# Opening an attention kernel over 256-row pieces of its input, with delayed value sums, the gate as a 129th value column, and four SSM input buffers

## The chip, the cores and the metric

The kernel runs on one core of a Trainium2 chip. The metric is the device time in microseconds (us) from start to end of one execution on that core; lower is better. Several executions of each kernel were timed.

Engines are named as the profile names them: PE is the matrix engine (TensorE), PEld its weight loads, DVE is VectorE, ACT is ScalarE, POOL is GpSimd, and SP is the engine that only starts DMA transfers here.

## The reference

A sequence `x` of 2048 rows and 1024 columns goes through two blocks, and a gate per row mixes their results.

```python
# x: 1 x 2048 x 1024, bf16
g = sigmoid((x * gate_w).sum(-1, keepdims=True))      # one gate value per row
a = A(x)      # state-space block (SSM): Bu = x @ B_bar.T (complex), h[t] = Lam_bar*h[t-1] + Bu[t],
              # y = 2*Re(h @ C.T) + x*Dskip; 2048 steps, 1024 complex states
b = B(x)      # attention: x @ wqkv, 32 heads of 32, softmax(q k^T / sqrt(32)) v, @ wo
out = g * a + (1 - g) * b                             # 1 x 2048 x 1024, bf16
```

The attention has 32 x 2048 x 2048 scores, and every one needs an exponential. That is 134 million exponentials on ScalarE.

## The kernel before

All exponentials are done in 1024 ACTIVATE instructions of 128 x 1024 elements. Two of them make a *burst*: the scores of one group of four heads, 256 query rows against 256 key rows. There are 512 bursts. Everything else (projections, the whole SSM block, the output projection) is cut into pieces and placed between the bursts: `MM_PER_PERIOD = 4` matmuls of 512 columns per burst on PE ("dense slots"), and VectorE work as long as a *planned* time says that there is room.

```python
def build(self):
    ...
    start = [self.d_v(0, 0), self.d_qk(0, 1, 1), self.d_v(0, 1), self.d_qk(0, 1, 2), self.d_v(0, 2), self.d_qk(0, 1, 3), self.d_v(0, 3),
             self.d_qk(0, 0, 1)]                      # V, K, Q of the first four heads: 512-column pieces, one bank
    proj[0] = [self.d_qk(0, 0, 2), self.d_gate(), self.d_qk(0, 0, 3)]
    ...
    for p in range(NBURST):
        g, pg = divmod(p, 64)
        self.burst(p)                                 # PE: scores; ACT: two exponentials
        if p >= 2:
            self.pv(p - 2)                            # PE: value sums of the burst before last
        ...
        quota = 8 if start else MM_PER_PERIOD
        ...                                           # dense pieces until the quota is used
        limit = t0 + (period - 0.1 if ended is not None else period + PE_HEAD)
        while self.bg or self.bg2:                    # VectorE background work, by planned time
            ...
            c = src[0][0]                             # planned cost of the next operation
            st = max(self.dve_t, t0 + 0.3)
            if c > 0 and st + c > limit:
                break
            src.pop(0)[1]()
            if c > 0:
                self.dve_t = st + c
        ...
        if ended is not None:
            ended.evac()                              # VectorE: PSUM -> SBUF, after the background work
            self.dve_t = max(self.dve_t, t0 + period) + 0.75
```

VectorE executes in the order in which the operations are emitted, as the runs below show: a K eviction emitted behind two operations of parameter math started 0.57 us after its matmuls were through (the changed kernel), and one emitted ahead of such math 0.04 us after (a_spareK).

The gate is computed by dense work of its own, with a moving operand that is one column wide:

```python
    def d_gate(self):
        ...
                for tt in (2 * q, 2 * q + 1):
                    for a in range(8):
                        m = e.matmul(ps[:, 7, tt:tt + 1], xT[:, a, 128 * tt:128 * (tt + 1)], self.gwb[:, a:a + 1], start=(a == 0), stop=(a == 7))
```

## Time and profile before

The time before is 978.16 us, the median of 3 executions (978.06 to 978.17).

The first lines are from the profile's page: busy time, share of the span and instruction count of each engine; the clock granted to PE in 40 equal slices, in tenths of full speed; and the chain of work that ended last, by engine.

```profile
...
PE 935.0 (96%) x15432; PEld 487.9 (50%) x15432; DVE 522.9 (54%) x1206; ACT 944.7 (97%) x1034; POOL 8.4 (1%) x46
...
PEclk9989999999999999999999999999999999999997
...
ACT 90%; DVE 5%; PE 3%; SPq 1%; DMA 0%; issue 0%
...
```

PE and ACT look equally busy, at 96% and 97%. The chain decides between them: 90% of it is ACT. Two slices of the clock row stand out: the third (an 8, between 49 and 73 us) and the last (a 7).

The next view divides the execution into four stretches: opening, the next 22 us, the long middle, and the tail after the start of the last exponential. The columns after the length are busy us and instruction counts of the engines, then the mean granted clock, the share of the DMA engines, and GB/s.

```profile
...
core 0: us, PE busy (x) PEld busy (x) DVE busy (x) ACT busy (x) POOL busy (x), PEclk, DMA share, GB/s
12.93:40.37 27.44, 22.51 (x353) 14.43 (x351) 23.52 (x92) 17.54 (x19) 2.45 (x6) 1.00 1.18 201
40.37:62.40 22.03, 20.31 (x396) 11.48 (x395) 20.73 (x78) 18.97 (x21) 0.00 (x0) 0.77 0.99 136
62.40:965.80 903.40, 877.30 (x14566) 454.27 (x14565) 472.04 (x1010) 903.16 (x986) 3.27 (x18) 1.00 0.23 54
965.80:976.90 11.10, 5.27 (x44) 1.95 (x40) 4.87 (x22) 2.83 (x6) 0.00 (x0) 0.50 0.23 78
...
```

ACT is busy for 903.16 of 903.40 us in the long middle. Nothing can be saved there unless an exponential becomes cheaper. What can be saved lies at the edges: ACT is idle for 9.9 us of the opening, for 3 us of the next stretch (at a mean clock of 0.77), before 12.93 us, and in the tail (at a clock of 0.50).

The opening's pattern shows in the timeline. Each line gives start and duration in us, engine, source line, operation, operands, count and, in brackets, how long the engine sat idle and what released it.

```profile
...
15.89 1.89 PE L1295 MATMUL f_ps<-f_xT,f_wb 128*128 128x512 bf16 x8 [0.79 <-DVE f_V L1319]
...
17.82 0.69 DVE L1302 CAST f_K<-f_ps 128x512 bf16<-128x512 f32 x1 [0.46 <-PE f_ps L1295]
...
18.57 0.40 PE L1448 MATMUL f_ps<-f_Q,f_K 32*128 32x256 bf16 x8 [0.79 <-DVE f_K L1302]
...
19.01 1.94 ACT L1454 ACTIVATE f_pt<-f_ps 128x1024 bf16<-128x1024 f32 x2 [1.92 <-PE f_ps L1448]
...
```

PE projects 512 columns of K (1.89 us), VectorE empties the bank (0.69 us), PE makes the scores, and only then can ACT go on, after 1.92 us of idleness. Then V follows (1.95 us at 19.31), with the same bank.

The clock dips between 45.05 and 55.29 us. The same view at its start:

```profile
...
43.36 0.40 PE L1448 MATMUL f_ps<-f_Q,f_K 32*128 32x256 bf16 x8
...
44.11 0.94 PE L1329 MATMUL f_ps<-f_gwb,f_xT 128*128 128x1 bf16 x32
...
45.12 0.61 PE L1448 MATMUL f_ps<-f_Q,f_K 32*128 32x256 bf16 x8
...
```

The scores (8 matmuls) take 0.40 us before 45.05 us and 0.61 us after it. The gate's matmuls, 128x1 each, run just before. The stretch view of the 3.41 us ahead of the drop is instructive:

```profile
...
41.64:45.05 3.41, 3.41 (x113) 2.81 (x112) 3.23 (x11) 3.41 (x5) 0.00 (x0) 1.00 1.43 176
...
```

PE was busy for 3.41 of 3.41 us there (by the profile, which models when a matmul ends), and still the clock was half (0.50) from its end to 55.29 us. What was low was the work in it: the one-column matmuls start 0.025 to 0.027 us apart, and 512-column ones at full clock 0.215 us apart. Counting the columns of the matmuls that start in that window, each matmul weighted by the share of the 128 rows that it used, it holds 1952 columns; 512-column matmuls one after the other would move about 8100 (estimate from the 0.215 us).

### The profile page before, as it was taken

How to read it: one execution, taken by the hardware profiler on the slowest of the kernel's cores; microseconds unless marked ns; L12 is line 12 of the kernel's file. 1: busy time of each engine (PE TensorE's matmuls, PEld its weight loads, DVE VectorE, ACT ScalarE, POOL GpSimd, SP SyncE). 2: the span in 40 equal slices, each digit the busy share in tenths (PEclk: the TensorE clock that was granted, in tenths of full speed). 3: DMA queues.
4: the chain of work that ended last, by engine and by line, in shares of the span. 5: the costliest groups of instructions: out<-in, count | busy, mean ns of one | idle time of the engine just before them, and what ended most of it. 6: DMA issues, size and time to landing. Idle time of an engine off the chain costs nothing.

```text
span 976.9 us, 33704 instructions
## 1 busy us (share of the span) xinstructions
PE 935.0 (96%) x15432; PEld 487.9 (50%) x15432; DVE 522.9 (54%) x1206; ACT 944.7 (97%) x1034; POOL 8.4 (1%) x46
## 2 busy tenths in 40 slices
PE   7899999999999999999999999999999999889996
PEld 4544554554444464444644644444554446444442
DVE  4897789877778844511257711177765112232223
ACT  4789999999999999999999999999999999999996
POOL 2000000000000000000000000000000000000000
PEclk9989999999999999999999999999999999999997
DMA  9992312311135202130022201142101213123311
GB/s 213 183 137 44 45 21 50 65 24 40 40 69 98 56 5 45 35 80 29 8 48 58 53 26 44 35 91 55 36 5 41 92 37 104 53 85 109 114 58 60
DMA packets 157011, 60.89 MB, mean 62 GB/s; under 512 B 145600, under 2 KB 145600, under 8 KB 156864
## 3 DMA queue, kind: packets, MB, share of 16 engines
q1 hardware_dynamic: 153664, 57.89, 26.8%
q8 instruction: 122, 2.00, 0.9%
q10 hardware_dynamic: 3200, 0.80, 0.4%
q14 instruction: 25, 0.20, 0.1%
HBM read 16.79 MB, written 12.58 MB: 30 GB/s over the span
## 4 chain that ended last, share of the span: by engine, by line
ACT 90%; DVE 5%; PE 3%; SPq 1%; DMA 0%; issue 0%
ACT f_pt L1454 90%; DVE f_OT L1218 1%; PE f_ps L1313 1%; DVE f_OT L1214 1%; PE f_ps L1470 1%; DVE f_OT L1216 1%; SPq L1020 0%; PE f_ps L1295 0%; PE f_ps L1448 0%; DVE f_OT L1215 0%; DMA f_xT<-in_A_x_dram 0%; PE f_ps L1344 0%; DVE f_V L1319 0%; DVE f_Et L1220 0%; DVE f_K L1302 0%
## 5 line engine op out<-in xcount | busy, mean ns | idle before, releaser
L1454 ACT ACTIVATE f_pt<-f_ps 128x1024 bf16<-128x1024 f32 x1024 | 940.7, 1266 | 13.7 <-PE f_ps L1448 13.6
L1470 PEld LDWEIGHTS f_ps<-f_V,f_pt 128*128 128x128 bf16 x8192 | 239.0, 96 | 110.0 <-issue 106.4
L1470 PE MATMUL f_ps<-f_V,f_pt 128*128 128x33 bf16 x8192 | 291.4, 178 | 0.5 <-DVE f_On L1484 0.5
L1448 PE MATMUL f_ps<-f_Q,f_K 32*128 32x256 bf16 x4096 | 204.2, 274 | 27.4 <-ACT f_pt L1454 8.0
L1448 PEld LDWEIGHTS f_ps<-f_Q,f_K 32*128 32x128 bf16 x4096 | 60.6, 92 | 246.1 <-ACT f_pt L1454 238.3
L1344 PE MATMUL f_ps<-f_xT,f_wb 128*128 128x512 bf16 x512 | 131.0, 377 | 2.4 <-DVE f_ub L1348 0.9
L1295 PE MATMUL f_ps<-f_xT,f_wb 128*128 128x512 bf16 x496 | 128.2, 382 | 2.3 <-DVE f_V L1319 1.3
L1383 DVE TENSOR_SCALAR f_Ag<-f_ps,f_gcol 128x512 f32<-128x512 f32 x32 | 24.0, 750 | 139.8 <-PE f_ps L1368 139.8
L1244 DVE TENSOR_TENSOR_SCAN f_ht<-f_pf,f_init,f_ut 128x512 bf16<-128x512 f32 x64 | 80.4, 1273 | 0.0
L1368 PE MATMUL f_ps<-f_cT_re,f_hp 128*128 128x512 bf16 x192 | 72.8, 379 | 0.3
L1368 PE MATMUL f_ps<-f_cT_im,f_hp 128*128 128x512 bf16 x192 | 72.6, 378 | 0.0
L1348 DVE CAST f_ub<-f_ps 128x512 bf16<-128x512 f32 x64 | 44.3, 691 | 51.9 <-PE f_ps L1344 51.8
L1313 PE MATMUL f_ps<-f_wb,f_xT 128*128 128x128 bf16 x1024 | 67.0, 219 | 0.0
L1401 PE MATMUL f_ps<-f_wb,f_OT 128*128 128x512 bf16 x252 | 65.9, 380 | 0.0
L1407 DVE SCALAR_TENSOR_TENSOR f_xT<-f_ps,f_gcol,f_hp 128x512 bf16<-128x512 f32 (+1 forms) x28 | 21.0, 751 | 76.2 <-PE f_ps L1401 76.2
L1313 PEld LDWEIGHTS f_ps<-f_wb,f_xT 128*128 128x128 bf16 x1024 | 57.6, 97 | 0.4 <-issue 0.2
L1344 PEld LDWEIGHTS f_ps<-f_xT,f_wb 128*128 128x128 bf16 x512 | 40.4, 96 | 34.5 <-issue 2.8
L1295 PEld LDWEIGHTS f_ps<-f_xT,f_wb 128*128 128x128 bf16 x496 | 39.4, 97 | 35.1 <-issue 2.1
L1302 DVE CAST f_Q<-f_ps 128x512 bf16<-128x512 f32 x31 | 21.4, 691 | 51.3 <-PE f_ps L1295 51.3
L1235 DVE TENSOR_TENSOR f_tq<-f_ub,f_Et 128x512 bf16<-128x512 bf16 x128 | 46.3, 419 | 0.1
L1235 DVE TENSOR_TENSOR f_tq<-f_ht,f_Et 128x512 bf16<-128x512 bf16 x128 | 46.3, 417 | 0.0
L1319 DVE CAST f_V<-f_ps 128x512 bf16<-128x512 f32 x32 | 22.2, 693 | 42.0 <-PE f_ps L1313 42.0
(114 smaller groups left out, 435.5 us busy)
## 6 DMA issues: line engine op xcount, KB each, us to landing
ag_scratch<-f_Ag SPq DMA_DIRECT2D x32, 256.0 KB, 2.0
f_hp<-ag_scratch SPq DMA_DIRECT2D x32, 256.0 KB, 2.7
f_wb<-in_B_wqkv_dram SPq DMA_DIRECT2D x21, 256.0 KB, 4.3
out_dram<-f_xT SPq DMA_DIRECT2D x16, 256.0 KB, 2.1
f_wb<-in_B_wo_dram SPq DMA_DIRECT2D x1, 1024.0 KB
f_OT<-f_On SPq DMA_TRANSPOSE x63, 2.4
f_wb<-in_B_wqkv_dram ACTq DMA_DIRECT2D x3, 256.0 KB, 3.8
f_wb<-in_B_wo_dram SPq DMA_DIRECT2D x1, 768.0 KB, 4.6
```

The lines of the kernel that those rows point to most:

```text
L1235: ops.append((c, lambda: dve(lambda e: e.tensor_tensor(o, a, b, op), r, w)))
L1244: ops.append((1.25, lambda ri=ri: dve(lambda e: e.tensor_tensor_scan(ht[:, ri, :], rr, ut[:, ri, :], self.init[:, ri, j:j + 1], ALU.mult, ...
L1295: mms.append((1, lambda e, f, l, a=a: e.matmul(ps[:, bank, :], w[:, g % 2, part, a, :], xT[:, a, 512 * ch:512 * (ch + 1)], start=f, stop=l ...
L1313: m = e.matmul(ps[:, bank, 128 * q:128 * (q + 1)], xT[:, a, 128 * kt:128 * (kt + 1)], w[:, g % 2, 2, a, :], start=(a == 0), stop=(a == 7))
L1344: mms.append((1, lambda e, f, l, a=a: e.matmul(ps[:, 7, :], bT[:, n % 2, ri, a, :], xT[:, a, 512 * ch:512 * (ch + 1)], start=f, stop=l), [ ...
L1348: self.dve(lambda e: e.tensor_copy(self.ub[:, n % 2, ri, :], ps[:, 7, :]), [("bank", 7)], [("ub", n % 2, ri)], "evac_u")
L1368: mms.append((1, lambda e, f, l, j=j, ri=ri: e.matmul(ps[:, 7, :], hp[:, ri, j, cols], cT[ri][:, j, 512 * cb:512 * (cb + 1)], start=f, sto ...
L1383: self.dve(lambda e: e.tensor_scalar(a, ps[:, 7, :], self.gcol[:, 0, tt:tt + 1], None, ALU.mult), [("bank", 7), "g0"], [at], "evac_c")
L1401: mms.append((1, lambda e, f, l, j=j: e.matmul(ps[:, 7, :], OT[:, j, 256 * qb + 128 * r:256 * qb + 128 * (r + 1)], wo[j][0][:, 512 * cb:51 ...
L1448: m = e.matmul(ps[:, 2 * sl[h // 2] + h % 2, 256 * kl:256 * (kl + 1)], K[32 * h:32 * h + 32, g % 2, 128 * kt:128 * (kt + 1)], Q[32 * h:32 ...
L1454: self.act(lambda e, s=s, p=p: e.activation(pt[:, p], ps[:, 2 * s:2 * s + 2, :], ACT.Exp, scale=SCALE), [("S", s)], [("pt", p)], "exp")
L1470: m = e.matmul(ps[:, 6, o:o + 33], pt[:, p, h2, 256 * kl + 128 * qt:256 * kl + 128 * (qt + 1)], V[:, g % 2, 2 * i + kl, h, :], start=(i == ...
```

## The change

The intent is to start ACT earlier and keep it fed, by five things:

1. K and V of the first four heads are projected in 256-row pieces, as `x` lands, so that bursts 0 to 8 can follow the pieces. All value sums are held back until burst 8 has been issued, so PE has less to do per piece. This needs 12 more tiles for exponentials, found in memory that is not used yet.
2. The gate weights become a 129th column of the value weights; the separate gate matmuls go.
3. Four instead of two input buffers (`ub`) for the first 16 SSM items.
4. The last four output matmuls ("rest") move from burst 508 to bursts 510 and 511, two in each.
5. The parameter math of the SSM is placed between the pieces of the opening, 0.7 us of it (planned) after each V eviction.

The core of the diff:

```diff
+REST = 510
...
-        self.ub = T("ub", [128, 2, 2, 512], BF)
+        ub = T("ub", [128, 2, 2, 512], BF)
+        self.ub = [ub[:, 0], ub[:, 1]] + [self.OT[:, 3, 1024 * k:1024 * (k + 1)].rearrange("p (r n) -> p r n", r=2) for k in range(2)]
...
-        for q in range(4):
-            self.ld_x(128 * q, 128 * (q + 1), ("x0", q))
-        for ch in range(1, 4):
-            self.ld_x(512 * ch, 512 * (ch + 1), ("x", ch))
...
+        self.ld_x(0)
...
+        for i in range(1, 8):
+            self.ld_x(i)
...
-            for k in range(16):
+            for k in range(12):
                 m = e.matmul(self.ps[:, 5, :], warm[:, 0:128], warm, start=True, stop=True)
...
+    OPENING = ("K0 B0 K1 M B1 Va0 Vb0 K2 Va1 B2 Vb1 K3 Va2 B3 Vb2 K4 Va3 B4 Vb3 K5 Va4 B5 Vb4 K6 Va5 B6 Q1 Vb5 "
+               "K7 Va6 B7 Vb6 Va7 Vb7 B8 G P0 P1 P2 B9 P3 P4 P5")
...
+            elif op in ("Va", "Vb"):
...
+                        m = e.matmul(ps[:, bank, 129 * h:129 * (h + 1)], xT[:, a, 128 * kt:128 * (kt + 1)], self.wv0[:, a, 0:129], start=(a == 0), stop=(a == 7))
...
+                if h:
...                                                     # V eviction, gate column eviction
+                    self.spare(0.7)
...
+    def spare(self, us):
+        while self.nmath and us > 0:
+            us -= self.bg2[0][0]
+            self.nmath -= 1
+            self.bg2.pop(0)[1]()
...
-    def d_gate(self):
...
+    def ub_of(self, n):
+        return n % 4 if n < 16 else n % 2
...
-        start = [self.d_v(0, 0), self.d_qk(0, 1, 1), ... , self.d_qk(0, 0, 1)]
+        start = [self.d_qk(0, 0, 1)]
-        proj[0] = [self.d_qk(0, 0, 2), self.d_gate(), self.d_qk(0, 0, 3)]
+        proj[0] = [self.d_qk(0, 0, 2), self.d_qk(0, 0, 3)]
...
-        seq += [(508, 6, r, cb, "rest") for r, cb in rcb]
+        seq += [(REST, 6, r, cb, "rest") for r, cb in rcb]
...
-        for p in range(NBURST):
+        pvs = {10: [6, 7], 11: [8, 9]}
+        for p in range(first, NBURST):                  # first = 10
...
+            if outs and outs[0][0] == REST and p >= REST and cur is None:
+                c = outs.pop(0)[1]
+                c.pieces[0][1]()
+                c.evac()
...
-                                u_ok = ri == 1 or (self.items_done >= n - 1 and hp_free)
+                                u_ok = ri == 1 or (self.items_done >= n - (3 if n < 18 else 1) and hp_free)
```

In the string `OPENING`, K, Q, Va and Vb are projections of a piece (V in two halves), B is a burst, P a value sum, M the transposition of the SSM parameters, and G the gate. The order of PE's instructions is exactly the order of this string.

## The prediction

> **What bounds the kernel now.** ScalarE. In the chain of waits 90% of the span is the exponential ACTIVATE (1024 of them, 940.7 us busy by the groups of instructions). Their starts, 12.93 to 965.77 us, lie 0.917 us apart on average after the 200th; a burst (two) costs 1.83 us. Only gaps, the time before the first and the tail can be saved. From the timeline:
> - before the first exponential: 12.93 us;
> - bursts 1 to 9: about 10.9 us over the cadence, because PE projects V and K (1.9 us each, 512 columns) and waits for a VectorE eviction (0.69 us) of one shared bank between bursts. Burst 8 starts at 37.69 us;
> - bursts 13 to 19: 3.8 us. The granted clock is 0.5 from 45.05 to 55.29 us, after the gate matmuls began (42.5 us, moving operand one column wide);
> - 66 to 964 us: about 2 us of small gaps;
> - tail: 11.1 us from the last exponential's start, again at clock 0.5 (from 963.2 us, after bursts with one output matmul each).
>
> [...] Counting moved columns weighted by the share of rows used, the windows before the two drops hold about 1950 and 3100[...].
>
> **What the change does.**
> 1. Opening: bursts 0 to 7 follow the 256-row pieces of x, value sums wait. Per piece PE does K (estimate 0.9 us, half of 1.9), V (0.9), scores (0.32): 2.1 us. The x transposes land between 6.7 and 24.3 us now (landings in the trace): about 2.4 us per piece, so arrival paces it. Burst 7's exponential comes about 2 us after the last landing (projection 0.9, eviction 0.45, scores 0.4, latencies): 26.3 us; burst 8 about 28.3 us instead of 37.69, without the 0.85 us gap after it. Saves 10 us, on ScalarE's critical path. The ten delayed value sums (0.45 us each) fit in the four ScalarE-bound bursts that follow.
> 2. Gate: 128 one-column matmuls and their eviction go; value columns grow from 128 to 129, which costs nothing visible. If the activity reading is right, the half-clock interval goes too: saves 3.8 us.
> 3. Four SSM buffers keep dense slots filled while VectorE (over 90% busy until 66 us) lags. Off the critical path: 0.
> 4. Rest of the output at bursts 510 and 511, two matmuls per burst: the clock should stay full for most of the tail, saving about 1 us.
>
> Sum 14.8 us: 963.4 us. I take 964, for evictions queued behind the parameter math.
>
> **Range.** 960.5 to 970. Faster by over 2% (below 958.6) 0.04; within 2% 0.95; slower 0.01.
>
> **What would show it.** First exponential near 10 us; burst 8 near 28 us; gaps afterwards under 5 us in sum; no clock of 0.5 between 40 and 60 us; PE released by x landings in the opening rather than by VectorE; the same 0.917 us cadence; last exponential near 952 us, tail near 10 us.
>
> **What would make it wrong.** In the opening PE waits for x; the window from 7.5 to 10.9 us may hold only about 3450 weighted columns, and the warm-up loses four matmuls. A drop there would cost about 5 us (estimate: 10 us at half clock). The last x piece could land later, as the value weights now load beside x. An eviction stuck behind math delays a burst. An idle stretch of dense work later could trip the clock again, about 4 us each.

The sum: 10 + 3.8 + 0 + 1 = 14.8 us, from 978.2 us to 963.4 us. The two drops are those of the kernel before, at 45.05 and 963.23 us; "windows" are stretches of 3.41 us ahead of them, a third of the 10.24 us at half clock and a twelfth of the 40.96 us at full clock ahead of it. "The activity reading" is that few weighted columns in a window (1950 and 3100 there) bring the drop. It was my estimate from these two drops, and the 3.8 us of term 2, the 1 us of term 4 and what the risks say of the clock rest on it.

## More of the kernel before

Within a burst the background operations go in first and the eviction that frees PE's bank goes in last. The only thing that keeps this from delaying PE is the planned cost `c`. For the tables of the SSM (`table_ops`, eight of them, 20 small operations each) the plan is:

```python
    for l in range(4, 9):
        n = 1 << l
        c = 0.08 + n / 960.0                          # planned us, the same for both kinds of operation
        ...
        add(c, lambda e, ...: e.tensor_scalar(ta[:, 0:n], si, wi, None, ALU.mult), ...)
        add(c, lambda e, ...: e.tensor_scalar(tb[:, 0:n], si, wr, None, ALU.mult), ...)
        add(c, lambda e, ...: e.scalar_tensor_tensor(dr, sr, wr, ta[:, 0:n], ALU.mult, ALU.subtract), ...)
        add(c, lambda e, ...: e.scalar_tensor_tensor(di, sr, wi, tb[:, 0:n], ALU.mult, ALU.add), ...)
```

## The result and the profile after

The changed kernel takes 975.14 us, the median of 4 executions (974.94 to 975.83); the kernel before takes 978.11 us (977.78 to 978.17) in the same rounds. The ratio is 0.9972, with a 95% interval from 0.9954 to 0.9989. Ratios here are the mean time of one kernel's fast runs over that of the other's fast runs of the same rounds, so they are not quite the ratio of the medians. The change is real but worth 3 us, not 14: the result lies above the range that I gave.

The profiled executions span 976.93 and 974.11 us, 2.82 us apart, so the two traces can be compared stretch by stretch. (The profiled execution of the changed kernel is its slowest of the four, by about 0.6 us.) The page of the changed kernel:

```profile
...
PE 929.2 (95%) x15308; PEld 486.4 (50%) x15308; DVE 524.5 (54%) x1223; ACT 944.5 (97%) x1034; POOL 8.2 (1%) x46
...
PEclk9999999999999999999999999999999999999996
...
ACT 85%; PE 7%; DVE 6%; DMA 1%; issue 1%; SPq 0%
...
```

The 8 in the third slice of the clock row is gone, as predicted. But the chain has moved: ACT fell from 90% to 85%, and PE and DVE together rose from 8% to 13%. There is more time in which ACT waits for a chain through the two others. The four stretches (the second ends at 62 us here):

```profile
...
9.67:34.43 24.76, 20.82 (x330) 16.51 (x330) 13.87 (x53) 17.64 (x22) 2.92 (x8) 1.00 1.17 203
34.43:62.00 27.57, 22.92 (x421) 11.96 (x418) 23.92 (x99) 24.41 (x29) 0.00 (x0) 1.00 1.08 155
62.00:961.55 899.55, 872.56 (x14467) 451.93 (x14464) 480.44 (x1048) 897.78 (x979) 3.33 (x18) 1.00 0.22 54
961.55:974.10 12.55, 6.28 (x58) 2.57 (x54) 5.59 (x23) 2.76 (x6) 0.00 (x0) 0.50 0.25 90
...
```

The second stretch has the full clock now, yet ACT is idle for 3.2 us of it (24.41 of 27.57). Before, it was idle for 3.1 us at a mean clock of 0.77. The tail, from the start of the last exponential, has grown from 11.16 to 12.55 us (the line for the kernel before starts 0.03 us after it).

I put landmarks on both traces by the starts of the exponentials. "Gaps" are what the distance from one exponential to the next exceeds its median of 0.913 us by, summed over distances at least 0.06 us too long. All in us:

| landmark | before | after | difference | predicted |
|---|---|---|---|---|
| first exponential | 12.93 | 9.67 | -3.26 | "near 10 us" |
| burst 8 starts | 37.69 | 32.50 | -5.19 | -9.4 |
| burst 9 starts | 40.37 | 34.43 | -5.94 | -10 |
| from burst 9 to the last exponential | 925.40 | 927.12 | +1.72 | -3.8 |
| of it, gaps of bursts 10 to 24 | 3.79 | 3.82 | +0.03 | -3.8 |
| of it, gaps of bursts 25 to 110 | 1.41 | 2.93 | +1.52 | 0 |
| of it, gaps of bursts 508 to 511 | 0.21 | 0.92 | +0.71 | 0 |
| tail, from the start of the last exponential | 11.16 | 12.55 | +1.39 | -1 |
| span | 976.93 | 974.11 | -2.82 | -14.8 |

Three places fail, by about 4, 5.5 and 2.5 us: the opening gained less than it should, the middle gained nothing where the half clock vanished, and the end grew. The traces suggest a reason for each.

**The opening.** The timeline of one piece in the changed kernel:

```profile
...
16.35 1.03 PE L1109 MATMUL f_ps<-f_xT,f_wb 128*128 128x256 bf16 x8
...
17.25 0.38 DVE L1220 SCALAR_TENSOR_TENSOR f_OT<-f_OT 128x208 f32<-128x208 f32 x1
17.66 0.37 DVE L1221 SCALAR_TENSOR_TENSOR f_OT<-f_OT 128x208 f32<-128x208 f32 x1
17.95 0.42 DVE L1121 CAST f_K<-f_ps 128x256 bf16<-128x256 f32 x1
...
18.43 0.40 PE L1527 MATMUL f_ps<-f_Q,f_K 32*128 32x256 bf16 x8 [0.57 <-DVE f_K L1121]
...
18.88 1.02 ACT L1533 ACTIVATE f_OT<-f_ps 128x1024 bf16<-128x1024 f32 x1 [0.95 <-PE f_ps L1527]
...
```

The K matmuls of the piece start at 16.35 us and are through at 17.38. The eviction of K (L1121) starts at 17.95 us: two operations of the parameter math stand in front of it. PE waits 0.57 us for it, and ACT 0.95 us for the scores. The waits of PE from 5 to 32 us, in total, by what ended them:

```profile
...
PE f_ps L1527 <- DVE f_K L1121: 3.0, 6, 0.8
PE f_ps L1098 <- DMA f_xT<-in_A_x_dram: 1.2, 1, 1.2
PE f_ps L1109 <- DMA f_xT<-in_A_x_dram: 0.7, 1, 0.7
...
```

K evictions cost PE 3.0 us in six waits. The `x` transposes cost 1.9 us in two waits at the very start, and none later. VectorE took its operations in order here: the eviction starts 0.29 us after the start of the last operation ahead of it (17.66 and 17.95 us), and 0.57 us after its input was complete.

**Bursts 10 to 24.** The second stretch shows the same thing with other operations:

```profile
...
42.30 0.25 DVE L1304 TENSOR_SCALAR f_OT<-f_OT,f_W 128x64 f32<-128x64 f32 x1
42.46 0.68 DVE L1392 CAST f_Q<-f_ps 128x512 bf16<-128x512 f32 x1
...
43.20 1.04 PE L1385 MATMUL f_ps<-f_xT,f_wb 128*128 128x512 bf16 x4 [1.30 <-DVE f_Q L1392]
...
44.62 1.02 ACT L1533 ACTIVATE f_pt<-f_ps 128x1024 bf16<-128x1024 f32 x1 [0.93 <-PE f_ps L1527]
...
```

Here a Q eviction sits behind operations of `table_ops` (L1303 to L1307, one after the other without a pause; the last ahead of it is shown); PE waits 1.30 us, and ACT 0.93 us. PE's waits from 34 to 66 us:

```profile
...
PE f_ps L1385 <- DVE f_Q L1392: 1.6, 2, 1.3
PE f_ps L1415 <- DVE f_rc L1562: 1.4, 1, 1.4
PE f_ps L1415 <- DVE f_ub L1421: 1.3, 1, 1.3
```

The three ACT gaps of over 1 us (bursts 14, 18 and 22: 1.14, 1.28 and 1.19 us) fall beside these waits and make up 3.61 of the 3.82 us. (The second line names a reciprocal, but a Q eviction ran just ahead of it on DVE, from 51.16 to 51.85 us, and PE went on at 51.99.)

**The end.** By the kernel's own schedule the last full output block is finished in burst 506, and the rest is not allowed before burst 510. PE's dense slots stay empty in bursts 507 to 509:

```profile
...
953.76 0.40 PE L1527 MATMUL f_ps<-f_Q,f_K 32*128 32x256 bf16 x8 [0.94 <-ACT f_pt L1533]
...
955.60 0.40 PE L1527 MATMUL f_ps<-f_Q,f_K 32*128 32x256 bf16 x8 [0.94 <-ACT f_pt L1533]
...
```

These are the scores of two bursts. Between them stand only value sums, and PE is idle for 0.94 us. The window from 952.9 to 956.3 us holds 2080 weighted columns, and the clock is half from 956.3 us to the end. Then the rest comes in pairs, and the second of a pair must wait until the bank is free of the first:

```profile
...
958.62 0.75 DVE L1483 SCALAR_TENSOR_TENSOR f_xT<-f_ps,f_gcol,f_xT 128x512 bf16<-128x512 f32 x1 [5.97 <-PE f_ps L1477]
...
959.43 0.61 PE L1477 MATMUL f_ps<-f_wb,f_OT 128*128 128x512 bf16 x1 [0.39 <-DVE f_xT L1483]
...
960.63 1.94 ACT L1533 ACTIVATE f_pt<-f_ps 128x1024 bf16<-128x1024 f32 x2 [0.51 <-PE f_ps L1527]
...
```

All of this is inference from one trace each. The experiments test it.

### The profile page after: what moved, and what is told of

It reads as the page before. It is cut to its first block, busy times and chain, and to the rows that moved or that the text cites. A ratio compares the mean times of both kernels' runs of the same rounds, so it can differ in the third digit from the quotient of the medians.

```text
span 974.1 us, 33474 instructions
## 1 busy us (share of the span) xinstructions
PE 929.2 (95%) x15308; PEld 486.4 (50%) x15308; DVE 524.5 (54%) x1223; ACT 944.5 (97%) x1034; POOL 8.2 (1%) x46
## 4 chain that ended last, share of the span: by engine, by line
ACT 85%; PE 7%; DVE 6%; DMA 1%; issue 1%; SPq 0%
ACT f_pt L1533 85%; PE f_ps L1415 2%; PE f_ps L1549 1%; PE f_ps L1527 1%; PE f_ps L1403 1%; DVE f_OT L1303 1%; DVE f_OT L1307 1%; DMA f_xT<-in_A_x_dram 1%; PE f_ps L1385 1%; DVE f_OT L1305 1%; DVE f_OT L1304 0%; PE f_ps L1145 0%; ACT f_Et L1533 0%; SPq L1031 0%; DVE f_hp L1325 0%
## 5 line engine op out<-in xcount | busy, mean ns | idle before, releaser
L1533 ACT ACTIVATE f_pt<-f_ps 128x1024 bf16<-128x1024 f32 x1012 | 929.0, 1258 | 7.3 <-PE f_ps L1527 7.3
L1549 PEld LDWEIGHTS f_ps<-f_V,f_pt 128*128 128x128 bf16 x8096 | 236.2, 96 | 106.9 <-issue 102.9
L1549 PE MATMUL f_ps<-f_V,f_pt 128*128 128x33 bf16 x8096 | 287.4, 178 | 0.1
L1415 PE MATMUL f_ps<-f_xT,f_wb 128*128 128x512 bf16 x512 | 131.0, 377 | 5.7 <-DVE f_ub L1421 2.2
L1385 PE MATMUL f_ps<-f_xT,f_wb 128*128 128x512 bf16 x472 | 121.2, 378 | 2.2 <-DVE f_Q L1392 2.2
L1477 PE MATMUL f_ps<-f_wb,f_OT 128*128 128x512 bf16 x252 | 66.5, 382 | 1.1 <-DVE f_xT L1483 1.1
L1403 PE MATMUL f_ps<-f_wb,f_xT 128*128 128x128 bf16 x896 | 59.2, 219 | 0.7 <-DVE f_K L1392 0.7
L1415 PEld LDWEIGHTS f_ps<-f_xT,f_wb 128*128 128x128 bf16 x512 | 40.5, 96 | 38.6 <-issue 5.7
L1421 DVE CAST f_ub<-f_ps 128x512 bf16<-128x512 f32 x48 | 33.2, 692 | 39.5 <-PE f_ps L1415 39.5
L1385 PEld LDWEIGHTS f_ps<-f_xT,f_wb 128*128 128x128 bf16 x472 | 36.8, 96 | 31.1 <-DVE f_Q L1392 2.5
L1403 PEld LDWEIGHTS f_ps<-f_wb,f_xT 128*128 128x128 bf16 x896 | 50.4, 97 | 1.2 <-DVE f_K L1392 0.8
L1562 DVE RECIPROCAL f_rc<-f_ps 128x8 f32<-128x8 f32 x63 | 13.1, 208 | 57.3 <-PE f_ps L1549 55.7
L1325 DVE TENSOR_TENSOR f_ut<-f_tq 128x512 f32<-128x512 bf16 x64 | 41.5, 685 | 0.0
```

The source lines that it names most:

```text
L1325: ops.append((c, lambda: dve(lambda e: e.tensor_tensor(o, a, b, op), r, w)))
L1385: mms.append((1, lambda e, f, l, a=a: e.matmul(ps[:, bank, :], w[:, g % 2, part, a, :], xT[:, a, 512 * ch:512 * (ch + 1)], start=f, stop=l ...
L1403: m = e.matmul(ps[:, bank, 128 * q:128 * (q + 1)], xT[:, a, 128 * kt:128 * (kt + 1)], w[:, g % 2, 2, a, :], start=(a == 0), stop=(a == 7))
L1415: mms.append((1, lambda e, f, l, a=a: e.matmul(ps[:, 7, :], bT[:, n % 2, ri, a, :], xT[:, a, 512 * ch:512 * (ch + 1)], start=f, stop=l), [ ...
L1421: self.dve(lambda e: e.tensor_copy(self.ub[k][:, ri, :], ps[:, 7, :]), [("bank", 7)], [("ub", k, ri)] + over, "evac_u")
L1477: mms.append((1, lambda e, f, l, j=j: e.matmul(ps[:, 7, :], OT[:, j, 256 * qb + 128 * r:256 * qb + 128 * (r + 1)], wo[j][0][:, 512 * cb:51 ...
```

## The experiments

Besides the change, twelve kernels ran, in four batches. All gave correct results, and none was faster or slower than the kernel before by 2%. The unchanged kernel's median moved between 977.4 and 979.1 us from batch to batch, so ratios are compared across batches and not times. Names that begin with `b_` are edits of the kernel before, those with `a_` of the changed kernel.

| run | median us | before, same rounds | ratio | 95% interval |
|---|---|---|---|---|
| the change | 975.14 | 978.11 | 0.9972 | 0.9954 to 0.9989 |
| a_nomath | 973.80 | 978.81 | 0.9947 | 0.9930 to 0.9963 |
| b_wide | 979.75 | 978.81 | 1.0012 | 0.9996 to 1.0029 |
| a_rest4 | 973.12 | 978.81 | 0.9945 | 0.9929 to 0.9962 |
| a_cost3 | 972.36 | 978.81 | 0.9934 | 0.9917 to 0.9951 |
| a_spareK | 973.60 | 979.11 | 0.9946 | 0.9929 to 0.9963 |
| b_cost3 | 975.74 | 979.11 | 0.9969 | 0.9952 to 0.9986 |
| b_wcost3 | 975.03 | 979.11 | 0.9963 | 0.9947 to 0.9980 |
| a_rest1 | 972.74 | 979.11 | 0.9942 | 0.9925 to 0.9959 |
| a_open | 975.61 | 978.56 | 0.9971 | 0.9956 to 0.9986 |
| a_q1late | 976.39 | 978.56 | 0.9980 | 0.9964 to 0.9995 |
| combo | 971.47 | 978.56 | 0.9930 | 0.9916 to 0.9943 |
| combo2 | 969.54 | 977.43 | 0.9917 | 0.9904 to 0.9931 |

Since single steps are worth 1 to 4 us, the landmarks of each run's profiled execution say more than its total. B7 and B9 are the starts of bursts 7 and 9; the last column lists the intervals of half clock between the first burst and 950 us (starts in us, and length in brackets). In the rows below the first two, starts of exponentials stand up to 0.02 us later than `prof` prints them; gaps and spans are not touched by this.

| run | first exp | B7 | B9 | gaps 10 to 24 | 25 to 110 | 508 to 511 | tail | span | half clock |
|---|---|---|---|---|---|---|---|---|---|
| before | 12.93 | 35.00 | 40.37 | 3.79 | 1.41 | 0.21 | 11.16 | 976.93 | 45.0 (10.2) |
| the change | 9.67 | 30.66 | 34.43 | 3.82 | 2.93 | 0.92 | 12.55 | 974.11 | none |
| a_nomath | 9.70 | 29.68 | 33.45 | 1.03 | 6.05 | 0.58 | 11.99 | 972.88 | 11.9 (3.4), 66.5 (3.4), 233.7 (6.8) |
| a_spareK | 9.65 | 29.96 | 33.73 | 3.84 | 3.00 | 0.71 | 11.90 | 972.56 | 11.5 (3.4) |
| a_q1late | 9.81 | 29.93 | 34.80 | 3.82 | 2.94 | 0.92 | 12.25 | 974.19 | none |
| a_open | 10.12 | 28.65 | 32.72 | 6.10 | 3.01 | 0.71 | 11.57 | 973.51 | 40.1 (3.4) |
| b_wide | 13.33 | 35.49 | 40.86 | 5.29 | 1.44 | 0 | 10.30 | 977.85 | 55.7 (6.8) |
| b_cost3 | 13.11 | 34.29 | 38.80 | 2.62 | 3.56 | 0 | 10.04 | 974.48 | 45.7 (6.8), 216.4 (10.2) |
| b_wcost3 | 13.41 | 34.69 | 39.20 | 1.10 | 3.16 | 0 | 10.42 | 973.29 | 214.3 (10.2) |
| a_cost3 | 9.84 | 30.68 | 34.45 | 0.25 | 3.44 | 0.71 | 11.80 | 970.82 | 231.7 (3.4) |
| a_rest1 | 9.72 | 30.47 | 34.23 | 3.81 | 2.92 | 0.22 | 10.44 | 971.08 | none |
| a_rest4 | 9.73 | 30.54 | 34.31 | 3.82 | 3.00 | 0 | 10.54 | 971.04 | none |
| combo | 9.80 | 28.73 | 32.80 | 3.61 | 2.96 | 0 | 9.76 | 969.74 | 39.7 (6.8), 234.2 (3.4) |
| combo2 | 9.83 | 28.43 | 32.20 | 0.24 | 3.82 | 0 | 9.52 | 965.15 | none |

### The opening: is it the arrival of x, or evictions behind math?

The theory is that PE is released late by K evictions that stand behind parameter math in VectorE's order. The rival is that the landing of `x` paces the opening, as I had predicted, or that PE simply has more work per piece.

**a_nomath** takes all parameter math out of the opening (it is done later, with the tables):

```diff
     def spare(self, us):
-        while self.nmath and us > 0:
+        while False:
```

> The changed kernel with no parameter math on VectorE during the opening; it is done afterwards. Theory A (in the opening the K evictions wait about 0.5 us per piece behind that math, so VectorE order, not the landing of x, paces it): K evictions follow their projection at once, the bursts of the opening lie about 2.4 us apart instead of 2.7, burst 7 starts at about 27.5 us instead of 30.66. Rival B (x or PE's own work paces it): burst 7 within 0.7 us of 30.66. The math then delays tables and items: the saved time may be lost again between 35 and 110 us, so the total is expected between 972 and 975.

**a_spareK** keeps the math in the opening and only moves it behind the K eviction, for the pieces from the third on:

```diff
                 evac(self.K[:, 0, 256 * i:256 * (i + 1)], 7, ("K", 0, i // 2), i % 2 == 0)
+                if i >= 2:
+                    self.spare(0.7)
...
-                    self.spare(0.7)
+                    if i >= 6:
+                        self.spare(0.7)
```

> The changed kernel with each portion of parameter math put on VectorE's queue just after the K eviction of the next piece instead of just before it; same amount of math. Theory A (queue order of the K eviction behind the math paces the opening): bursts 3 to 6 lie 2.35 to 2.45 us apart as in the run without math (2.37), burst 7 starts 1.5 to 2.5 us earlier than 30.66 unless the clock drops near 11 us, and unlike there the gaps from burst 25 to 110 stay near 3 us, so time about 973. Rival B (the math's amount, not its place, fills VectorE): spacing stays above 2.6 us.

Measured: bursts 2 to 6 lie 2.36 to 2.37 us apart in both runs, as expected, against 2.64 to 2.89 us in the changed kernel. Burst 9 moved from 34.43 to 33.45 us (a_nomath) and 33.73 us (a_spareK), although both executions had 3.4 us of half clock at 11.5 or 11.9 us, which the changed kernel's had not. The forecasts for burst 7 were missed: it came at 29.68 us in a_nomath (27.5 expected) and 0.7 us earlier in a_spareK (1.5 to 2.5 expected unless the clock dropped). The step from burst 6 to 7 hardly changed (3.54 us, from 3.62); it holds Q1, which is tested next. What a_nomath gained, it partly lost again: its gaps of bursts 25 to 110 are 6.05 us. The timeline of a_spareK, one piece:

```profile
...
16.50 0.40 PE L1530 MATMUL f_ps<-f_Q,f_K 32*128 32x256 bf16 x8
...
17.31 1.03 PE L1109 MATMUL f_ps<-f_xT,f_wb 128*128 128x256 bf16 x8
...
18.38 0.42 DVE L1121 CAST f_K<-f_ps 128x256 bf16<-128x256 f32 x1 [0.38 <-PE f_ps L1109]
18.72 0.26 DVE L1222 TENSOR_SCALAR f_OT<-f_OT 128x208 f32<-128x208 f32 x1
...
18.86 0.40 PE L1530 MATMUL f_ps<-f_Q,f_K 32*128 32x256 bf16 x8
...
```

The eviction now starts as soon as the K matmuls are through, and math follows it. One piece takes 2.36 us (from scores at 16.50 to scores at 18.86), against those 2.64 to 2.89 us in the changed kernel. PE's waits for K fall from 3.0 us in six waits to one:

```profile
...
PE f_ps L1530 <- DVE f_K L1121: 0.4, 1, 0.4
```

What follows: from burst 2 to 6 the evictions behind math were the wait, and the landing of `x` was not. The run also corrects my figure for the work of a piece. I had added up issue times to 2.1 us. The piece is really a loop: scores to next K 0.81 us (16.50 to 17.31), then K projection, eviction and scores 1.55 us (17.31 to 18.86), and one of the two half V projections that I had counted as work (18.18 us) fits inside the latter. That is 2.36 us, as long as the 2.4 us between landings.

**a_q1late** tests a second omission. Burst 8 belongs to the next 256 query rows, and the changed kernel projects those (Q1, 8 matmuls of 256 columns, about 0.87 us) before burst 7; I had forgotten it in the sum. The edit moves it behind burst 7:

```diff
-    ... K6 Va5 B6 Q1 Vb5 K7 Va6 B7 Vb6 Va7 Vb7 B8 ...
+    ... K6 Va5 B6 Vb5 K7 Va6 B7 Q1 Vb6 Va7 Vb7 B8 ...
```

> The changed kernel with only the second query projection moved from before burst 7 to after it. Theory: it is 0.87 us of PE work in a PE-paced stretch that the prediction left out; burst 7 starts about 0.9 us earlier (29.8), but burst 8 then waits for it and for three value projections, so the start of burst 9 moves by less than 0.5 us and the time stays within 0.7 us of the changed kernel.

Measured: burst 7 came at 29.93 instead of 30.66 us, and burst 8 at 32.87 instead of 32.50 us; the time is 0.9980 of before, so nothing was gained. What follows: Q1 is 0.7 us of burst 7's lateness, but it has to be paid before burst 8, wherever it stands. It is work that the prediction left out, not a badly placed step.

**a_open** takes the opening as far as I could: a_spareK's order, three dummy matmuls of 512 columns to keep the clock up at 10 us, Q1 behind burst 7, the last V projections behind burst 8, and the value sums one burst later.

```diff
-    OPENING = ("K0 B0 K1 M ... K6 Va5 B6 Q1 Vb5 K7 Va6 B7 Vb6 Va7 Vb7 B8 G P0 P1 P2 B9 P3 P4 P5")
+    OPENING = ("K0 B0 W K1 M ... K6 Va5 B6 Vb5 K7 Va6 B7 Q1 Vb6 B8 Va7 Vb7 G P0 P1 B9 P2 P3 P4")   # W: 3 dummy matmuls
...
-        pvs = {10: [6, 7], 11: [8, 9]}
+        pvs = {10: [5, 6], 11: [7, 8], 12: [9, 10]}
```

> The changed kernel with all that seems wrong in its opening set right, the rest untouched: the math after the K evictions, the second query projection moved from before burst 7 to after it, two value projections and the value sums shifted by a burst, and three dummy matmuls while PE waits for the second piece of x so that the clock does not drop near 11 us. If PE's work per piece now paces the opening (2.37 us) up to the last piece: burst 7 at 26.5 to 28 us instead of 30.66, burst 8 at most 2.1 us later, no gap of 1.7 us before burst 7; the later gaps as in the changed kernel (3.8 and 2.9 us), time about 971. If the landing of the last piece (24.9 us in the changed kernel) binds, burst 7 stays at or above 27 us with PE waiting for x.

Measured: burst 7 at 28.65 us and burst 9 at 32.72 us, so the opening is 1.7 us shorter. Here the landing of `x` finally binds: the last piece landed at 26.57 us, 1.7 us later than in the changed kernel's execution; PE waits 0.87 us for it before the last K projection, which starts at 26.62 us, and burst 7 follows 2.03 us later. That is the "about 2 us after the last landing" of the prediction. But the time is 0.9971, no better than the change: gaps of bursts 10 to 24 went from 3.82 to 6.10 us. A value sum that now comes later waited 0.77 us for a normalization at 37.28 us, the window from 36.7 to 40.1 us was left with 2328 weighted columns, and the clock was half for the next 3.4 us, with a gap of 3.27 us at burst 13. Moving work out of the opening thinned out the window after it.

### Bursts 10 to 24: what was the half clock worth?

My prediction took the whole gap sum of 3.8 us for the cost of the half clock. The theory after the result: the plan of `table_ops` is too short, so evictions sit behind tables in either kernel, and at half clock PE was slow enough to hide that. In the traces a TENSOR_SCALAR of n elements takes about 0.13 + n/1920 us from start to start and a SCALAR_TENSOR_TENSOR about 0.26 + n/960 us (a fit; the medians stand below, at a_cost3), while the plan has 0.08 + n/960 for both. A table of 20 such operations and two copies is planned at 4.4 us, and takes 6.2 us. The rival: the half clock really cost 3.8 us, and something new in the changed kernel costs as much. The two factors can be switched one by one in the kernel *before*.

**b_wide** removes the cause of the drop alone. The gate's moving operand is made 32 columns wide, with 32 copies of the weights, so that the same 128 matmuls move 4096 columns instead of 128:

```diff
-        self.gwb = T("gwb", [128, 8], BF)
+        self.gwb = self.OT[:, 3, 0:256].rearrange("p (a n) -> p a n", a=8)
...
-        add(0.1, lambda e: e.tensor_copy(self.gwb[:], P(GW)), q(GW), ["gwb"])
+        add(0.1, lambda e: e.tensor_copy(self.gwb, P(GW).unsqueeze(2).to_broadcast([128, 8, 32])), q(GW), ["gwb"])
...
-                        m = e.matmul(ps[:, 7, tt:tt + 1], xT[...], self.gwb[:, a:a + 1], ...)
+                        m = e.matmul(ps[:, 7, 32 * tt:32 * (tt + 1)], xT[...], self.gwb[:, a, :], ...)
```

> The kernel before, with the gate's moving operand repeated to 32 columns: same number of matmuls and weight loads, same result, more moved columns. Theory A (the half clock from 45 to 55 us is set off by the nearly empty gate matmuls, and it alone costs the 3.8 us of gaps in bursts 13 to 19): no half clock before 963 us, those gaps under 1 us, time about 974.3. Rival B (the clock drop is real, but PE is also late because VectorE evictions wait behind table arithmetic; at half clock this was hidden): no half clock, but gaps of over 1.5 us in bursts 13 to 22 with PE released by VectorE evictions, time above 976. If the clock still drops, the low-activity reading is wrong.

Measured: 1.0012 of before, so nothing was gained, although the drop at 45 us is gone. That is rival B, but for a new drop later on. Instead there is one gap of 4.14 us at burst 17, and gaps of bursts 10 to 24 rose to 5.29 us. The timeline shows why:

```profile
...
56.42 0.68 DVE L1302 CAST f_Q<-f_ps 128x512 bf16<-128x512 f32 x1
...
57.63 1.48 PE L1344 MATMUL f_ps<-f_xT,f_wb 128*128 128x512 bf16 x3 [3.65 <-DVE f_OT L1218]
...
59.72 1.02 ACT L1454 ACTIVATE f_pt<-f_ps 128x1024 bf16<-128x1024 f32 x1 [3.94 <-PE f_ps L1448]
...
```

A Q eviction comes at 56.42 us, behind tables. PE, which needs its bank, was idle for 3.65 us, and ACT then for 3.94 us. (The profile names the operation that began after the eviction, L1218, as the releaser. By the times it was the eviction: it ends at 57.10 us, and PE's first weight load follows at 57.23.) And a drop of the clock follows that idleness: the window from 52.3 to 55.7 us holds 2064 weighted columns, and the clock is half from 55.7 to 62.6 us.

**b_cost3** corrects the planned costs alone, for the first three tables (with all eight corrected, the changed kernel's schedule, used below, does not come out; with three it does):

```diff
-            c = 0.08 + n / 960.0
+            ct, c = (0.13 + n / 1920.0, 0.26 + n / 960.0) if j < 3 else (0.08 + n / 960.0,) * 2
...
-            add(c, lambda e, ...: e.tensor_scalar(...), ...)      # both of them
+            add(ct, lambda e, ...: e.tensor_scalar(...), ...)
```

> The kernel before with the corrected VectorE costs of tables 0 to 2 and its narrow gate as it was. Theory A (two limits lie one behind the other there: the half clock, and evictions placed too late; removing one exposes the other): the half clock from about 45 us stays, the gaps of bursts 10 to 24 stay at 3 us or more (3.8 in the kernel before), time within 1.5 us of the kernel before. Rival B (the late evictions alone caused the gaps and the half clock cost nothing): gaps fall below 1.5 us, time 3 us less.

**b_wcost3** has both edits.

> Both at once in the kernel before: the gate widened to 32 columns and the corrected costs. Theory A: no half clock near 45 to 65 us, gaps of bursts 10 to 24 under 1 us (3.8 before, 5.3 with the wide gate alone), time 3 to 4 us below the kernel before. Rival B (VectorE's throughput is short and the gaps only move on): sum of the gaps from burst 10 to 110 within 1.5 us of the 5.2 us of the kernel before.

The four kernels form a square. Gaps of bursts 10 to 24, in us:

| | planned costs as they were | first three tables corrected |
|---|---|---|
| gate one column wide (half clock at 45 us) | 3.79 (before, 10.2 us at half clock) | 2.62 (b_cost3, 6.8 us) |
| gate 32 columns wide (no drop at 45 us) | 5.29 (b_wide, which drops at 55.7 us) | 1.10 (b_wcost3) |

With the plan as it was, taking the half clock away made this stretch worse by 1.5 us. With the plan corrected, taking it away made it better by 1.5 us. So the half clock is worth about 1.5 us here, not 3.8, and only once the evictions are not late. The totals agree in direction, but b_cost3 and b_wcost3 (0.9969 and 0.9963) are closer together than their intervals are wide, so the 1.5 us rest on the gaps of single executions. Nor does the square switch the clock cleanly: b_wide has a half clock of its own within these bursts.

b_wcost3 met theory A on the clock and, nearly, on the gaps (1.10 us, not under 1); its time is 4.1 us below that of the kernel before in the same rounds. But it met the mark of rival B as well: its gaps of bursts 10 to 110 sum to 4.26 us, only 0.94 less than the 5.20 of before. In the kernel before, part of what the edits gain in bursts 10 to 24 comes back later (1.41 us became 3.16 in bursts 25 to 110), so the square speaks for bursts 10 to 24 alone.

I missed with b_cost3. I had expected it to stay near the time of before, because the half clock would still hold the bursts up. It gained 3 us. About 1.6 us of that came in the opening (burst 9 at 38.80 us) and 1.1 us in the tail, where its clock was full again from 967.3 to 970.7 us, places that I hadn't thought of; the gaps of bursts 25 to 110 grew by 2.1 us, with a half clock at 216 us later.

**a_cost3** makes the same correction in the changed kernel, where the clock is full anyway. If the theory holds, the 3.8 us of gaps must go; if something else in the changed kernel makes them, they stay.

> The changed kernel with the plan's costs of the VectorE operations of tables 0 to 2 set to what the trace measured (6.2 us a table instead of 4.4), so that fewer are put ahead of an eviction. Theory A (the gaps of bursts 14 to 22, 3.8 us, come from evictions that the plan puts too late in VectorE's order): they fall below 1 us, and the time by about 3, to 972. Rival B (VectorE's throughput itself is short there; the gaps only move): the gaps between bursts 9 and 110 sum to within 1.5 us of the 6.8 us of the changed kernel, time within 1 us of 975.1.

Measured: gaps of bursts 10 to 24 fell from 3.82 to 0.25 us, and the time to 0.9934. Of PE's waits from 34 to 66 us, 4.3 us in the changed kernel, this is left:

```profile
...
PE f_ps L1415 <- DMA f_wb<-in_A_B_re_dram: 1.1, 1, 1.1
PE f_ps L1385 <- DVE f_Q L1392: 0.4, 1, 0.4
...
```

The first of these waits (at 65.11 us) makes a gap of 1.10 us at burst 26: with the evictions out of the way, the landing of SSM weights ends last there, and combo2, below, has 1.56 us at the same burst. The gaps of bursts 10 to 110 sum to 3.69 us, 3.06 less than in the changed kernel, so rival B fails here. The edit changes nothing but the planned costs. This settles the second failure: what remained after the half clock had gone were evictions behind underpriced table operations. The gain in time is not all from here, though. Of the 3.57 us, 0.5 came back in bursts 25 to 110 and 1.0 in bursts 111 to 507 (most of it at burst 117, where the clock was half). The end, in turn, was about 1 us shorter; there the clock was full again from 962.1 to 969.0 us, and not half throughout.

The plan's formula gives 0.10 us for 16 elements (0.08 + 16/960). In the trace of the kernel before a SCALAR_TENSOR_TENSOR of 16 elements took 0.23 us, and 0.26 us passed until the next started (44.60 and 44.86 us). Over the tables of that kernel, the medians from the start of an operation to the start of the next are these, in us:

| elements | 16 | 32 | 64 | 128 | 256 |
|---|---|---|---|---|---|
| TENSOR_SCALAR | 0.14 | 0.15 | 0.16 | 0.20 | 0.27 |
| 0.13 + n/1920 | 0.14 | 0.15 | 0.16 | 0.20 | 0.26 |
| SCALAR_TENSOR_TENSOR | 0.27 | 0.28 | 0.32 | 0.39 | 0.52 |
| 0.26 + n/960 | 0.28 | 0.29 | 0.33 | 0.39 | 0.53 |

The two slopes show in the durations as well: 0.28 us (TENSOR_SCALAR) and 0.35 us (SCALAR_TENSOR_TENSOR) at 128 elements became 0.35 and 0.48 us at 256.

### The end: the clock, or the placing of the rest?

Two things got worse at the end, and they come together: the clock was half from 956.3 us, and two rest matmuls with one bank were squeezed into each of the last two bursts.

**a_rest1** puts the rest back to one per burst from burst 508 on:

```diff
-REST = 510
+REST = 508
...
-            if outs and outs[0][0] == REST and p >= REST and cur is None:
-                c = outs.pop(0)[1]
-                c.pieces[0][1]()
-                c.evac()
```

**a_rest4** does the same and issues each rest matmul four times (with the same result), so that PE has more to do, to see whether the clock stays up longer.

```diff
+            rep = 4 if kind == "rest" else 1
+            ...                                       # each rest matmul rep times, start=f, stop=l
```

> The changed kernel with the rest of the output at bursts 508 to 511, one chain per burst as before, and each of these four matmuls issued four times over (same result) to keep PE active. Theory A (the drop to half clock at 956 us, set off by two bursts without dense work, costs the 0.9 us of gaps at bursts 510 and 511 and stretches the tail): the clock stays full past 960 us, those gaps vanish, from the start of the last exponential to the end 10 us instead of 12.5, time about 971.8. Rival B (the tail is set by the order of the rest matmuls and their evictions, not by the clock): about 973.8, as in the kernel before (11.1 us of tail).

> The changed kernel with the rest of the output at bursts 508 to 511, one chain per burst, without the fourfold repetition. It parts the place of these matmuls from the clock. If the gain of the fourfold run (span 3.1 us less than the changed kernel) came from the clock, this one drops to half clock at about 956 to 960 us and keeps a tail of 11 us or more, gaining 1 to 2 us; if it came from the place, it gains the same 3 us.

Measured: 0.9945 (a_rest4) and 0.9942 (a_rest1); spans of 971.04 and 971.08 us, 3.0 us less than the changed kernel's in both. The clock differed: a_rest4 kept it full until 967.1 us, and a_rest1 had half clock from 955.9 to 962.8 us, before the last exponentials had run. Both ended the gaps before the tail (0 and 0.22 us, from 0.92) and shortened the tail to about 10.5 us. What follows: undoing the move gives 3 us back, even where the clock still falls early. These two runs alone don't part the pairing from the clock, because a_rest1's clock was full again from 962.8 to 966.2 us, within its tail, and a_rest4 carries twelve extra matmuls. The other traces do, as far as single executions of different kernels can:

| tail, us | half clock throughout | half clock for part of the tail |
|---|---|---|
| rest in pairs at bursts 510 and 511 | 12.55 (the change), 12.25 (a_q1late) | 11.6 to 12.0 (a_open, a_cost3, a_spareK, a_nomath) |
| rest one per burst from 508 | 11.16 (before) | 9.5 to 10.4 (combo2, combo, b_cost3, b_wide, b_wcost3, a_rest1) |

At half clock throughout, the pairs cost 1.1 to 1.4 us of tail. The half clock itself is worth something of the same size: the tail is 0.3 to 1.6 us shorter where part of it ran at full clock. When the clock falls differs from run to run: at 963.2 us before, 956.3 us in the change, 955.9 us in a_rest1 and 967.1 us in a_rest4.

### Putting the corrections together

**combo** joins a_open's opening (with one burst's dense quota lowered to 2), corrected costs for the first four tables, and a_rest1's end.

> All at once: the opening as in a_open, the corrected VectorE costs of tables 0 to 3, the rest of the output at bursts 508 to 511 one per burst. If the gains add: burst 9 about 3 us earlier than in the changed kernel, gaps of bursts 10 to 24 under 1 us (3.8), tail 10.5 us (12.5): span about 964 to 966 and time 965 to 967. If VectorE's throughput takes part back, the gaps from burst 25 to 110 grow from 2.9 to 5 us or more and the time is 968 to 970.

Measured: 971.47 us, 0.9930. The thinned-out window after a_open's opening came back, with half clock at 39.7 us and 3.61 us of gaps. So I kept the original order of the value sums:

**combo2** is a_spareK, the three dummy matmuls, corrected costs for three tables and a_rest1:

```diff
-    OPENING = ("K0 B0 K1 M B1 ... 
+    OPENING = ("K0 B0 W K1 M B1 ...                   # the rest of the order as in the change
...                                                     # and the edits of a_spareK, a_cost3, a_rest1
```

> Only the parts that gained when tried alone: math after the K evictions with dummy matmuls while PE waits for the second piece of x, corrected VectorE costs of tables 0 to 2, rest of the output at bursts 508 to 511 one per burst; the order of queries and value sums as in the changed kernel. Theory (the loss of the combined run before came from its shifted value sums: a value sum waits for a normalization in burst 11, and the clock drops at 40 us): no half clock between 30 and 60 us, gaps of bursts 10 to 24 under 0.7 us, burst 9 at 31.5 to 33 us, tail under 11 us, span 966 to 968, time 967 to 969. Rival (VectorE takes it back): gaps over 2.5 us in bursts 10 to 24 or over 5 us in 25 to 110, time above 970.5.

Measured: 969.54 us, the median of 5 (966.99 to 971.16), against 977.43 us for before (977.00 to 980.13, 9 executions); the ratio is 0.9917 (0.9904 to 0.9931). It beats both kernels, and its interval lies below that of the change. The landmarks came as expected, or better; the median is 0.5 us above the expected 967 to 969 us. The profiled execution was the luckiest of the five, with the highest mean clock. Its stretches:

```profile
...
9.83:32.20 22.37, 21.50 (x333) 16.61 (x332) 14.12 (x53) 17.64 (x22) 2.82 (x8) 1.00 1.15 207
32.20:60.00 27.80, 26.89 (x483) 13.91 (x480) 23.17 (x84) 27.78 (x32) 0.00 (x0) 1.00 1.05 169
60.00:955.63 895.63, 868.56 (x14425) 450.56 (x14424) 482.31 (x1064) 893.65 (x976) 3.71 (x18) 1.00 0.22 54
955.63:965.15 9.52, 3.26 (x33) 1.38 (x28) 4.54 (x22) 3.05 (x6) 0.00 (x0) 0.84 0.27 91
...
```

In the second stretch ACT is busy for 27.78 of 27.80 us; in the changed kernel it was idle for 3.2 us there. The tail ran at a mean clock of 0.84 and took 9.52 us. In all, about 5.4 us of the missing 12 (0.9972 less 0.9917, of 978 us) are recovered by moving and pricing operations, without taking any work out.

## Why the prediction was wrong

- **"burst 8 about 28.3 us", "Saves 10 us": wrong.** The first exponential came as predicted (9.67 us), and `x` landed as predicted (the last piece 24.9 us after the start, 24.3 predicted). The step that failed is "2.1 us [...] about 2.4 us per piece, so arrival paces it". Two paces within 15% of each other were compared, and one of them was a sum of issue times. The loop through the K eviction takes 2.36 us (a_spareK), and with parameter math ahead of the eviction 2.64 to 2.89 us. In addition the sum left out Q1, 0.7 us of burst 7's lateness (a_q1late). Burst 7's scores are therefore tied to PE and VectorE, and the last K projection started 3.7 us after its data had landed. combo2, with evictions first and no drop, has burst 9 at 32.20 us: 2.2 of the 4 us come back. The other 1.8 us include Q1 (about 0.87 us of PE's work); the rest of them is not assigned.
- **"I take 964, for evictions queued behind the parameter math": the right mechanism, far too small.** I put 0.6 us on it. It measured 3.0 us of PE waits in the opening (2.2 us of time, by combo2), and the same mechanism with the tables another 3.6 us of gaps (a_cost3), of which about 1.5 us came back later.
- **"the half-clock interval goes too: saves 3.8 us": the first half was right, the second wrong.** Gate matmuls with one column went with the drop at 45 us (1952 columns in the window ahead of it): made wider, they left none there (b_wide, b_wcost3), and without them the changed kernel has none between 40 and 60 us. But I took the gaps in that stretch to be the clock's cost. The 2 x 2 shows about 1.5 us, in single executions, and only with the plan of VectorE corrected. Without that, PE at full clock runs into the late evictions, and the gaps stay (3.79 and 3.82 us).
- **"Four SSM buffers [...] 0".** Gaps of bursts 25 to 110 are 1.5 us longer in the changed kernel: at bursts 46, 56, 68, 78 and 88, where evictions of u, K or Q come late. The experiments do not separate the cause. A version of the changed kernel with two buffers was only built, not run: it leaves output work over at the end of the schedule. So this stays open.
- **"the clock should stay full for most of the tail, saving about 1 us": wrong in sign.** The tail and the four bursts before it cost 2.1 us more. I looked at the work that was moved *to* bursts 510 and 511 and not at the slots that it left: bursts 507 to 509 got no dense work, and the clock fell at 956.3 us, before the tail. How early it falls is partly luck: a_rest1, with bursts 508 and 509 filled again, fell at 955.9 us. Of the six traces with the rest in pairs, five fell 3.6 us or more before the last exponential; of the seven with one rest matmul per burst (a_rest4 aside), only a_rest1 did. And of two matmuls that share a bank, the second waited 0.39 and 0.30 us for the eviction of the first. a_rest1 and a_rest4 give 3.0 us of span back. That full clock shortens the tail was the right idea, by the table above; the move bought the opposite.
- **Right:** the first exponential; no added cost of the 129th column to speak of (0.059 us from start to start, against 0.056 with 128); the cadence; ACT as the bound of the long middle; the class "within 2%". A drop of the clock after an idle stretch was named as a risk, and it occurred, at the end (0.94 us of idle PE in each of two bursts, then half clock from 956.3 us).

The terms add up as follows. Predicted -14.8 us, measured -2.8 us in the profiled executions: opening -5.9 (not -10), bursts 10 to 24 0.0 (not -3.8), bursts 25 to 110 +1.5 (not 0), last bursts and tail +2.1 (not -1); the remaining -0.5 us is spread over the other bursts in differences too small to assign.

## What to carry to other kernels

When a stretch of low clock vanishes, ask what its slowness was hiding: what it is worth has to be read in a version where the next wait is gone too, and switching the two causes one by one in the old kernel shows it. On an engine that works in order, as VectorE did here, put the eviction that another engine waits for ahead of filler work (bursts 2.36 us apart instead of 2.64 to 2.89), and price the filler by measured start-to-start times, small operations above all (0.27 us at 16 elements where the plan had 0.10). Before you take a saving for granted because one stream paces a loop, add up the whole loop through the other engines, with its evictions, and look as well at the slots that a moved operation leaves empty.

## What the traces show of the clock and of small VectorE operations

- The half-clock intervals that ended before the kernel did were 3.41, 6.83 or 10.24 us long, one, two or three times 3.413 us, with a phase that differed from run to run: the drops at 45.05 us (before), 956.34 (the change), 955.9 (a_rest1) and 967.1 (a_rest4) lie 0.7, 0.6, 0.2 and 1.1 us after a multiple of 3.413 us. An idle PE isn't needed for a drop. In the kernel before, PE was busy for 3.41 of 3.41 us in the window ahead of the drop at 45.05 us, with matmuls of one column.
- The work in a window goes with the drop. The windows of each trace were laid from its own drops, and the columns of the matmuls that start in a window were counted, times the share of the 128 rows in use. In the fourteen traces, all 23 full-clock windows under 2500 columns (those with a whole window after them) were followed by half clock (1952, 2064, 2080 and 2328 among them), and none over 3104 was. From 2592 to 3104 both occurred, 8 times half clock and 15 times not. In the kernel before, for one, 3104 columns at 959.8 us were followed by half clock, and 3104 at 956.4 us were not. Time that PE was busy doesn't part the windows: 3.41 of 3.41 us ahead of the drop at 45.05 us, and 2.69 of 3.42 us in the window before that one, which no half clock followed. That is a fit to these traces, not a known rule. In this count a matmul with 32 rows, as the scores have, weighs a quarter.
- Short idle times were enough for a drop: gaps of 0.94 us in each of two bursts, in which nothing but scores and value sums ran (953 to 956 us in the changed kernel, 2080 columns), came before the half clock at 956.3 us.
- The small operations of the tables cost more than the plan had: a SCALAR_TENSOR_TENSOR of 16 elements 0.26 us from start to start (44.60 and 44.86 us, kernel before), against 0.10 us. TENSOR_SCALARs of 16 elements follow each other after 0.14 us although each takes 0.23 us.
